# A factor per hidden column: multiplied into the weights, or applied to h as it leaves PSUM

## The chip, the cores and the metric

The kernel runs on one core of one Trainium2 chip. The metric is the device time of one execution in microseconds. A profile's span is about 1.8 us shorter than the device time of the same execution. The engines are TensorE (PE; PEld is its weight load), VectorE (DVE), ScalarE (ACT), GpSimd (POOL) and SyncE (SP; SPq is its queue of transfers).

## The reference, cut to what matters

```python
# attention: batch 8, heads 8, seq 576, head_dim 64; k and v averaged in pools of 8
attn = softmax(scale * q @ k_p^T);  x = (attn @ v_p)          # 4608 tokens x 512
# feed forward: w_in 512 x 2048, w_out 2048 x 512, alpha 2048
h = x @ w_in
s = np.sin(alpha * h)
g = h + s * s / (alpha + 1e-09)
return g @ w_out
```

Everything is float32. The kernel multiplies g by (alpha + 1e-9) and divides the rows of w_out by the same factor. What it forms is therefore (alpha + 1e-9) h + sin²(alpha h), and the question is where that one multiplication by alpha + 1e-9 happens.

## The kernel before

The kernel before scales the columns of w_in, 16 DVE operations, three ahead of the first unit and the others in it, so PSUM already holds the scaled h:

```python
def combine_w_in(self, J, part):                  # J = 0..3; parts 0 and 1
    ...
    def scaled(t, i):
        c = self.alb[:, i * h + J * w:i * h + (J + 1) * w].unsqueeze(1).to_broadcast([P, 2, w])
        nc.vector.tensor_tensor(out=t[:, :, s], in0=t[:, :, s], in1=c, op=OP.mult)
    ...                                           # scaled() for four blocks, then sums of blocks
```

`alb` is alpha + 1e-9 broadcast over the partitions, made at the start with four matmuls. The hidden layer is a product of 2x2 blocks with seven products in place of eight. Tokens come in nine **units** of 512. A unit has four **groups** of 256 hidden columns (J), and a group has seven products, so a unit has 28 **slots**, 0 to 27, of one product each. What a group does after product k stands in the functions `left0` to `left6`:

```python
def left2(G=G, Q=before):                         # Q is the group before
    if Q: self.store_g(Q)                         # SyncE: 1 MB to the bridge tensor in HBM
    G.b7 = bank(); nc.scalar.copy(out=G.b7[:], in_=G.b6[:])
    G.p5 = self.tp.tile([P, JW, TH], F32, name="p5")
    nc.scalar.copy(out=G.p5[:], in_=G.b5[:])      # 128x512
def left3(G=G):
    sin(G, 0, 0, G.b1); square(G, G.s[:, 0, 0])   # Sin with a scale per partition
def left4(G=G): add(G.g[:, 1, 1], G.b7[:], G.p5[:])
def left5(G=G):
    add(G.g[:, 0, 1], G.b6[:], G.p5[:])
    sin(G, 1, 1, G.g[:, 1, 1])
    add(G.g[:, 0, 0], G.b1[:], G.s[:, 0, 0])
```

`G.g` has two buffers, which take turns, and is what `store_g` sends. Beside the hidden products the attention of the **next** batch is made, in fixed slots:

```python
for i in range(5):                                # five tiles of tokens, units 1 to 6
    at((1, 3, 4, 5, 6)[i], A.score, i)            # PE; DVE takes max and subtracts it
    at(8 + (i + 1) // 2, A.exp, i)                # ACT
    at(9 + (i + 1) // 2, A.norm, i)               # DVE sums, GpSimd multiplies
    at((12, 12, 13, 14, 14)[i], A.turn, i)        # DVE transposes blocks into tr
at(14, A.move, 0); at(15, A.move, 1)              # SyncE: aT <- tr, 2 x 6 transfers
...
    at(24, A.values, hp)                          # four products of aT with v; ACT copies them into x
at(24, A.values_rest)
...                                               # turn_q, DVE, writes tr again from slot 21 on
```

Score tiles, and the products with v, share a ring of three PSUM buffers.

## Time and profile before

| | us |
|---|---|
| median of the runs (957.71 to 959.04) | 958.2 |
| span of the profile | 956.4 |
| first hidden product | 38.2 |
| unit 0 | 38.2 to 115.3 |
| units 1 to 6, sum | 343.0 |
| mean of units 1 to 5 | 57.22 |

A unit is measured in the trace from the start of the first matmul of its first product to the same in the next unit; all unit and slot times below are worked out so. Three things are to be read from the profile before: PE is full from unit 1 on, DVE bounds the last half of unit 0, and units 1 to 6 have almost the same length. The lines that carry this are in the prediction.

### The profile page before, as it was taken

Reading aid. Unit: us, or ns where it says so; the run is one execution under the profiler, and the core shown is the slowest. Engines: PE = TensorE matmul, PEld = TensorE weight load, DVE = VectorE, ACT = ScalarE, POOL = GpSimd, SP = SyncE. Lnnn points to the kernel's source line nnn. Section 1 sums busy time; section 2 is a strip of 40 time slices with the busy share of each in tenths; the row PEclk is TensorE's granted clock in tenths of the full one; section 3 lists DMA queues with packets and bytes.
Section 4 is the critical chain, followed back from the end, with each engine's and each line's share of the span. In section 5 each row is a group of like instructions: output and inputs, shape, how many; then the busy total and the mean of one; then the engine's idle time right before and its main releaser. Section 6 shows DMA issues by size and latency. Waiting matters only on the chain.

```text
span 956.4 us, 18152 instructions
## 1 busy us (share of the span) xinstructions
PE 937.6 (98%) x7259; PEld 833.4 (87%) x7259; DVE 676.5 (71%) x1070; ACT 414.2 (43%) x919; POOL 197.7 (21%) x215
## 2 busy tenths in 40 slices
PE   7998999999999999999999999999999999999998
PEld 3677687887878878787888899999999999999998
DVE  5889585766838577483576996867768695958684
ACT  5376466575756747566555531111111111111111
POOL 1717364443724436260000000000000000000000
PEclk9999999999999999999999999999999999999999
DMA  9636466666576663745615235324142434343201
GB/s 222 176 104 198 125 195 142 205 149 196 171 198 201 156 190 102 188 136 161 242 54 206 98 142 190 125 102 161 67 155 78 143 115 147 98 139 122 100 34 35
DMA packets 84038, 137.88 MB, mean 144 GB/s; under 512 B 10177, under 2 KB 49873, under 8 KB 79345
## 3 DMA queue, kind: packets, MB, share of 16 engines
q1 hardware_dynamic: 83920, 136.70, 47.1%
q8 instruction: 58, 0.95, 0.4%
q14 instruction: 26, 0.21, 0.1%
q10 hardware_dynamic: 34, 0.02, 0.0%
HBM read 74.47 MB, written 47.19 MB: 127 GB/s over the span
## 4 chain that ended last, share of the span: by engine, by line
PE 92%; DVE 4%; ACT 2%; DMA 1%; issue 0%; SPq 0%; DVEq 0%; ACTq 0%
PE bank L489 42%; PE bank L752 30%; PE ps_y L752 12%; PE ps_o L309 3%; PE ps_sc L208 2%; DMA q<-in_q_dram 1%; DVE as L368 1%; ACT s L495 1%; PE ps_at L267 1%; DVE home L462 1%; DVE a L372 1%; PE ps_qt L189 1%; PE bank L452 1%; DVE h L468 0%; PE ps_or L318 0%
## 5 line engine op out<-in xcount | busy, mean ns | idle before, releaser
L489 PE MATMUL bank<-home,a 128*128 128x256 f32 x1152 | 266.3, 382 | 3.0 <-DVE h L468 1.6
L489 PEld LDWEIGHTS bank<-home,a 128*128 128x128 f32 x1152 | 215.3, 190 | 36.6 <-DVE h L468 3.1
L489 PE MATMUL bank<-home,as 128*128 128x256 f32 x864 | 201.6, 382 | 2.8 <-DVE as L368 1.6
L489 PEld LDWEIGHTS bank<-home,as 128*128 128x128 f32 x864 | 161.7, 190 | 26.7 <-ACT bank L507 2.4
L105 POOL TENSOR_TENSOR kvin<-kvin 72x512 f32<-72x512 f32 x112 | 126.0, 1125 | 180.3 <-DMA kvin<-in_v_dram 112.0
L495 ACT ACTIVATE s<-h,rat 128x256 f32<-128x256 f32 x144 | 65.2, 500 | 90.2 <-DVE h L468 90.2
L468 DVE TENSOR_TENSOR h<-bank,p 128x512 f32<-128x512 f32 x72 | 49.1, 682 | 74.7 <-ACT s L497 47.4
L752 PE MATMUL bank<-wb,home 128*128 128x128 f32 x712 | 92.1, 275 | 0.0
L752 PEld LDWEIGHTS bank<-wb,home 128*128 128x128 f32 x712 | 85.7, 192 | 0.0
L831 ACT COPY bank<-bank 128x128 f32<-128x128 f32 x63 | 15.8, 250 | 149.3 <-PE bank L752 149.2
L497 ACT ACTIVATE s<-s 128x512 f32<-128x512 f32 (+1 forms) x106 | 77.8, 768 | 1.1
L495 ACT ACTIVATE s<-bank,rat 128x256 f32<-128x256 f32 x144 | 59.9, 467 | 36.9 <-PE bank L489 24.4
L752 PE MATMUL bank<-wb,xe 128*128 128x128 f32 x512 | 67.6, 275 | 0.0
L752 PEld LDWEIGHTS bank<-wb,xe 128*128 128x128 f32 x512 | 62.4, 192 | 0.1
L844 ACT COPY bank<-bank 128x128 f32<-128x128 f32 x63 | 15.8, 250 | 96.6 <-PE bank L752 96.6
L250 POOL TENSOR_TENSOR ex<-ex,sm 128x576 f32<-128x576 f32 (+1 forms) x38 | 42.5, 1148 | 46.5 <-DVE sm L249 21.4
L549 DVE TENSOR_TENSOR h<-h,s 128x1024 f32<-128x1024 f32 x36 | 44.5, 1237 | 0.0
L549 DVE TENSOR_TENSOR h<-bank,s 128x512 f32<-128x512 f32 x36 | 24.5, 681 | 24.5 <-ACT s L497 23.9
L819 ACT COPY bank<-ps_y 128x256 f32<-128x256 f32 x63 | 22.5, 357 | 35.9 <-PE ps_y L752 35.9
L519 ACT COPY bank<-bank 128x512 f32<-128x512 f32 x36 | 20.6, 571 | 39.4 <-PE bank L489 39.4
L712 DVE TENSOR_TENSOR xe<-home 128x512 f32<-128x512 f32 x30 | 19.4, 687 | 25.5 <-PE bank L752 25.4
L215 DVE TENSOR_REDUCE mx<-ps_sc 128x4 f32<-128x288 f32 (+1 forms) x75 | 33.6, 448 | 4.4 <-PE ps_sc L208 4.4
(152 smaller groups left out, 1499.3 us busy)
## 6 DMA issues: line engine op xcount, KB each, us to landing
g_bridge<-h SPq DMA_DIRECT2D x36, 1024.0 KB
r<-g_bridge SPq DMA_DIRECT2D x18, 1024.0 KB
home<-g_bridge SPq DMA_DIRECT2D x18, 1024.0 KB
out_dram<-o SPq DMA_DIRECT2D x36, 256.0 KB
q<-in_q_dram SPq DMA_DIRECT2D x8, 1024.0 KB
kvin<-in_k_dram SPq DMA_DIRECT2D x28, 288.0 KB
kvin<-in_v_dram SPq DMA_DIRECT2D x28, 288.0 KB
a<-in_moe_w_in_dram SPq DMA_DIRECT2D x16, 256.0 KB
```

The lines of the kernel that those rows point to most:

```text
L105: (eng or nc.gpsimd).tensor_tensor(out=o, in0=t[:, :, 0:w], in1=t[:, :, w:2 * w], op=OP.add)
L215: nc.vector.tensor_reduce(out=mx[:n], in_=ps[:n], axis=AX, op=OP.max)
L250: eng.tensor_tensor(out=E(n, i, 0, H), in0=E(n, i, 0, H), in1=sm[:n].unsqueeze(2).to_broadcast([n, H, Sp]), op=OP.mult)
L309: nc.tensor.matmul(ps[64 * e:64 * e + 64, :], vp[:, h, :], x, start=True, stop=True)
L468: add = lambda o, x, y: nc.vector.tensor_tensor(out=o, in0=x, in1=y, op=OP.add)
L489: nc.tensor.matmul(ps[:, jj, :], self.A[p][:, kk, f * P:(f + 1) * P], x[:, kk, :], start=(start and jj == 0 and kk == 0), stop=(kk == 1), ...
L495: nc.scalar.activation(out=G.s[:, i, j, jj, :], in_=src[:, jj, :], func=AF.Sin, scale=self.rat[:, f:f + 1])
L497: square = lambda G, x: nc.scalar.activation(out=x, in_=x, func=AF.Square)
L519: nc.scalar.copy(out=G.b7[:], in_=G.b6[:])
L549: add = lambda o, x, y: nc.vector.tensor_tensor(out=o, in0=x, in1=y, op=OP.add)
L752: nc.tensor.matmul(out, A[:, J, :], W[:, J // 2, J % 2, :], start=(start and J == 0), stop=(J == self.NJ - 1), skip_group_check=True)
L819: nc.scalar.copy(out=x[:, 0:2, :], in_=yz[:, 0:1, :].to_broadcast([P, 2, P]))
```

## The change

The intent: take the 16 scalings, and the broadcast of alpha, out of the start, where DVE is the bound. In their place ACT's copies of one PSUM bank and DVE's adds, which read PSUM anyway, take alpha + 1e-9 as a scale per partition. Five groups of slots were moved too. The diff, cut to its core:

```diff
-    def load_alpha(self, row, rows): ...     # alb: alpha + 1e-9 broadcast over partitions
+    def load_alpha(self, rows): ...          # al, ale = al + 1e-9, ral = 1/ale, rat = al/ale
...
 def combine_w_in(self, J, part):
-        def scaled(t, i): ...                # and its 16 uses
...
             def left2(G=G, Q=before):
-                G.p5 = self.tp.tile([P, JW, TH], F32, name="p5")
-                nc.scalar.copy(out=G.p5[:], in_=G.b5[:])
+                for i in (1, 0):
+                    for jj in range(JW):
+                        f = self.chunk(G, i, jj)
+                        nc.scalar.activation(out=G.g[:, i, 1, jj, :], in_=G.b5[:, jj, :], func=AF.Identity, scale=self.ale[:, f:f + 1])
...
             def left4(G=G):
-                add(G.g[:, 1, 1], G.b7[:], G.p5[:])
+                self.scale_add(G, 1, 1, G.b7, G.g[:, 1, 1])
...                                           # the other two adds, and one in finish(), the same way
+    def scale_add(self, G, i, j, h, x):
+        for jj in range(JW):
+            f = self.chunk(G, i, jj)
+            self.nc.vector.scalar_tensor_tensor(out=G.g[:, i, j, jj, :], in0=h[:, jj, :], scalar=self.ale[:, f:f + 1],
+                                                in1=x[:, jj, :], op0=OP.mult, op1=OP.add)
...                                           # unit 0
-            at(6, A.k_t)
+            at(7, A.k_t)
-                at((7, 8, 9, 11, 13)[i], A.score, i)
+                at((8, 9, 10, 11, 13)[i], A.score, i)
...                                           # units 1 to 6
-                at(9 + (i + 1) // 2, A.norm, i)
-                at((12, 12, 13, 14, 14)[i], A.turn, i)
+                at((9, 10, 10, 12, 12)[i], A.norm, i)
+                at((13, 13, 13, 14, 14)[i], A.turn, i)
...
-                at(24, A.values, hp)
-            at(24, A.values_rest)
+                at(24 + hp // 2, A.values, hp)
+            at(25, A.values_rest)
```

More of the change, by code (lines that the diff above doesn't have):

```diff
@@ L321, in attention, with load_alpha, turn_alpha @@
         return SimpleNamespace(**{f.__name__: f for f in (k_t, q_t, score, exp, score_exp, norm, new_a, a_t, turn, move, values, values_rest)})
-    def load_alpha(self, row, rows):
+    def load_alpha(self, rows):
         nc = self.nc
-        self.al = self.const.tile([P, self.K2], F32, name="al")
-        self.ral = self.const.tile([P, self.K2], F32, name="ral")
-        self.rat = self.const.tile([P, self.K2], F32, name="rat")
-        self.alb = self.new_tr()[:, 0:self.FF]
-        self.al_row, self.al_rows = row[0:1], rows[:self.K2]
+        self.al, self.ale, self.ral, self.rat = (self.const.tile([P, self.K2], F32, name=n) for n in ("al", "ale", "ral", "rat"))
+        self.al_rows = rows[:self.K2]
         nc.scalar.dma_start(out=self.al_rows, in_=self.alpha.rearrange("(k p) -> k p", p=P))
-        nc.scalar.dma_start(out=self.al_row, in_=self.alpha.rearrange("(o n) -> o n", o=1))
-    def combine_alpha(self):
+    def turn_alpha(self):
         nc = self.nc
@@ L340, in combine_alpha @@
         nc.scalar.copy(out=self.al[:], in_=ps[:])
-        for c in range(4):
-            s = slice(512 * c, 512 * c + 512)
-            ps = self.bank([P, 512], c)
-            nc.tensor.matmul(ps[:], self.ones[:], self.al_row[:, s], start=True, stop=True)
-            nc.scalar.activation(out=self.alb[:, s], in_=ps[:], func=AF.Identity, bias=self.ex[:, 0, 0, self.Sp:self.Sp + 1])
-        nc.vector.tensor_scalar(out=self.ral[:], in0=self.al[:], scalar1=1e-9, scalar2=None, op0=OP.add)
-        nc.vector.reciprocal(out=self.ral[:], in_=self.ral[:])
+        nc.vector.tensor_scalar(out=self.ale[:], in0=self.al[:], scalar1=1e-9, scalar2=None, op0=OP.add)
+        nc.vector.reciprocal(out=self.ral[:], in_=self.ale[:])
         nc.vector.tensor_tensor(out=self.rat[:], in0=self.al[:], in1=self.ral[:], op=OP.mult)
@@ L368, in combine_w_in @@
         tt = lambda o, x, y, op: nc.vector.tensor_tensor(out=o[:, :, s], in0=x[:, :, s], in1=y[:, :, s], op=op)
-        def scaled(t, i):
-            c = self.alb[:, i * h + J * w:i * h + (J + 1) * w].unsqueeze(1).to_broadcast([P, 2, w])
-            nc.vector.tensor_tensor(out=t[:, :, s], in0=t[:, :, s], in1=c, op=OP.mult)
-        if J < 2:
-            if part == 0:
-                scaled(a11, 0)
-                scaled(a21, 1)
-                scaled(a22, 1)
-                tt(s1, a21, a22, OP.add)
-            else:
-                tt(s2, s1, a11, OP.subtract)
-                scaled(a12, 0)
-                tt(a21, a11, a21, OP.subtract)
-                tt(s4, a12, s2, OP.subtract)
-        elif part == 0:
-            for t, i in ((a11, 0), (a21, 1), (a22, 1), (a12, 0)):
-                scaled(t, i)
+        if part == 0:
+            tt(s1, a21, a22, OP.add)
         else:
-            tt(s1, a21, a22, OP.add)
             tt(s2, s1, a11, OP.subtract)
@@ L490, in product, with sin @@
                                          start=(start and jj == 0 and kk == 0), stop=(kk == 1), skip_group_check=True)
-            def sin(G, i, j, src):
+            def sin(G, i, j, src, by):
                 for jj in range(JW):
-                    f = i * self.K2 // 2 + G.J * JW + jj
-                    nc.scalar.activation(out=G.s[:, i, j, jj, :], in_=src[:, jj, :], func=AF.Sin, scale=self.rat[:, f:f + 1])
+                    f = self.chunk(G, i, jj)
+                    nc.scalar.activation(out=G.s[:, i, j, jj, :], in_=src[:, jj, :], func=AF.Sin, scale=by[:, f:f + 1])
             square = lambda G, x: nc.scalar.activation(out=x, in_=x, func=AF.Square)
@@ L519, in left2 @@
                 nc.scalar.copy(out=G.b7[:], in_=G.b6[:])
-                G.p5 = self.tp.tile([P, JW, TH], F32, name="p5")
-                nc.scalar.copy(out=G.p5[:], in_=G.b5[:])
+                for i in (1, 0):
+                    for jj in range(JW):
+                        f = self.chunk(G, i, jj)
+                        nc.scalar.activation(out=G.g[:, i, 1, jj, :], in_=G.b5[:, jj, :], func=AF.Identity, scale=self.ale[:, f:f + 1])
             def left3(G=G):
-                sin(G, 0, 0, G.b1)
+                sin(G, 0, 0, G.b1, self.al)
                 square(G, G.s[:, 0, 0])
             def left4(G=G):
-                add(G.g[:, 1, 1], G.b7[:], G.p5[:])
+                self.scale_add(G, 1, 1, G.b7, G.g[:, 1, 1])
             def left5(G=G):
-                add(G.g[:, 0, 1], G.b6[:], G.p5[:])
-                sin(G, 1, 1, G.g[:, 1, 1])
-                add(G.g[:, 0, 0], G.b1[:], G.s[:, 0, 0])
+                self.scale_add(G, 0, 1, G.b6, G.g[:, 0, 1])
+                sin(G, 1, 1, G.g[:, 1, 1], self.rat)
+                self.scale_add(G, 0, 0, G.b1, G.s[:, 0, 0])
             def left6(G=G):
-                sin(G, 0, 1, G.g[:, 0, 1])
-                sin(G, 1, 0, G.b7)
+                sin(G, 0, 1, G.g[:, 0, 1], self.rat)
+                sin(G, 1, 0, G.b7, self.al)
                 if early(G):
@@ L547, in finish, with chunk @@
     def finish(self, Q):
-        nc = self.nc
-        add = lambda o, x, y: nc.vector.tensor_tensor(out=o, in0=x, in1=y, op=OP.add)
-        add(Q.g[:, 1, 0], Q.b7[:], Q.s[:, 1, 0])
-        add(Q.g[:, :, 1], Q.g[:, :, 1], Q.s[:, :, 1])
+        self.scale_add(Q, 1, 0, Q.b7, Q.s[:, 1, 0])
+        self.nc.vector.tensor_tensor(out=Q.g[:, :, 1], in0=Q.g[:, :, 1], in1=Q.s[:, :, 1], op=OP.add)
+    def chunk(self, G, i, jj):
+        return i * self.K2 // 2 + G.J * JW + jj
+    def scale_add(self, G, i, j, h, x):
+        for jj in range(JW):
+            f = self.chunk(G, i, jj)
+            self.nc.vector.scalar_tensor_tensor(out=G.g[:, i, j, jj, :], in0=h[:, jj, :], scalar=self.ale[:, f:f + 1],
+                                                in1=x[:, jj, :], op0=OP.mult, op1=OP.add)
     def store_g(self, Q):
@@ L572, in first_batch @@
         h = [self.hp.tile([P, 4 * POOL * self.D], F32, name="h") for _ in range(2)]
-        self.load_alpha(h[1][:], self.hp.tile([P, P], F32, name="s", bufs=1)[:])
-        self.combine_alpha()
+        self.load_alpha(self.hp.tile([P, P], F32, name="s", bufs=1)[:])
+        self.turn_alpha()
         for i in range(4):
@@ L858, in run @@
             make_identity(nc, ident)
-            self.ones = const.tile([1, P], F32, name="ones")
-            nc.gpsimd.memset(self.ones[:], 1.0)
             engines = {nc.tensor.engine, nc.vector.engine, nc.scalar.engine, nc.gpsimd.engine, nc.sync.engine}
```

## The prediction

> **What bounds the kernel now.** I read the strips of the page first, then the chain that ended last, then the sums by stretch, and last the order of time on TensorE (PE), VectorE (DVE) and ScalarE (ACT) in the stretch that looked worst. From the page:
>
> ```profile
> PE 937.6 (98%) x7259; PEld 833.4 (87%) x7259; DVE 676.5 (71%) x1070; ACT 414.2 (43%) x919; POOL 197.7 (21%) x215
> ...
> PE   7998999999999999999999999999999999999998
> PEld 3677687887878878787888899999999999999998
> DVE  5889585766838577483576996867768695958684
> ...
> PE 92%; DVE 4%; ACT 2%; DMA 1%; issue 0%; SPq 0%; DVEq 0%; ACTq 0%
> ```
>
> PE is busy nearly always and makes 92% of the chain; what is not PE lies in the first five slices (a slice is 24 us), where DVE reaches 8 and 9. So the kernel has three stages: a start up to about 115 us, hidden products on PE up to about 560 us, output products after that. The sums by stretch (columns: PE, PEld, DVE, ACT, POOL busy) say how they differ:
>
> ```profile
> 62.89:80.92 18.03, 17.03 (x154) 13.88 (x148) 17.53 (x31) 8.98 (x19) 6.09 (x7) 1.00 0.79 234
> 80.92:98.36 17.44, 13.79 (x73) 11.39 (x73) 16.71 (x24) 13.85 (x24) 14.51 (x13) 1.00 0.48 132
> 98.36:113.61 15.25, 15.25 (x94) 10.62 (x93) 7.76 (x11) 7.23 (x19) 6.33 (x8) 1.00 0.42 129
> 113.61:300.00 186.39, 186.39 (x1442) 152.37 (x1441) 125.23 (x216) 117.03 (x230) 85.80 (x93) 1.00 0.66 179
> ```
>
> From 62.89 to 98.36 DVE is busy 34.2 of 35.5 us: it is the bound there. After 113.61 PE has no idle time, DVE is at 67% and ACT at 63%. In that stage one product of the hidden layer is 8 matmuls, and two in a row take 3.45 us from start to start, so 1.73 each. A unit of 512 tokens is 28 products; its stores to the bridge tensor come 57.2 to 57.5 us apart. The first unit takes from 38.21 to 115.3, that is 77.1 us. It does more: ten groups of transposes of the attention (about 0.43 each), five of q (0.55), the leftovers of batch 0 (about 1.4), 8.5 in all. 57.3 + 8.5 = 65.8, so **PE loses about 11.3 us in the first unit**. That is all a relief of DVE and ACT could win.
>
> **What the Trainium skill says, and whether the trace agrees.**
> "VectorE: DVE Perf Modes", section on the TRN2 errata: a float32 tensor_tensor takes (N+151)/0.96 ns, so 691 for 512 and 424 for 256; the trace has 682 and 415. It gives no figure for scalar_tensor_tensor; I take it as a tensor_tensor of its size.
> The same table: ScalarE from PSUM takes (172+FD)/1.2 ns, so 357 for 256 and 570 for 512. The trace has 357 and 571 for plain copies, but 467 for a Sin of 256 whose scale is read per partition, and 687 for an Identity of 512 with a bias read per partition: about 110 more.
> "SBUF — State Buffer", section "SBUF: two separate sides": a DVE operation with two SBUF inputs and a GpSimd operation that reads SBUF exclude each other for a whole instruction. The trace agrees: four scalings of w_in took 2.49 us at one place and 4.56 at another where GpSimd was busy. The new fused operation reads one input from PSUM, so by this it is not held up.
> "ScalarE: Activation LUTs", "Table sets: the hidden batching unit": cheap functions, identity among them, are in every set. The two kernels' lists of instructions agree: both have 16 table loads, so the new Identity adds none.
>
> **The change, part by part.** The times by line, shapes kept apart (count | busy us, mean ns):
>
> ```profile
> L495 ACT ACTIVATE s<-bank,rat 128x256 f32<-128x256 f32 x144 | 59.9, 467 | 36.9 <-PE bank L489 24.4 <-issue 8.8 <-DVE h L549 1.2
> L468 DVE TENSOR_TENSOR h<-bank,p 128x512 f32<-128x512 f32 x72 | 49.1, 682 | 74.7 <-ACT s L497 47.4 <-PE bank L489 20.0 <-issue 6.6
> L521 ACT COPY p<-bank 128x512 f32<-128x512 f32 x36 | 21.2, 589 | 0.0
> L372 DVE TENSOR_TENSOR a<-a,tr 128x512 f32<-128x512 f32 x16 | 12.7, 842 | 0.0
> ```
>
> 1. Removed on DVE: the 16 scalings of w_in, 12.7 us (mean 842, against 0.62 where GpSimd is quiet), all before 84.1 us.
> 2. Removed at the very start: 4 broadcasts of alpha through PE (7.2 us) and 4 ACT activations (2.7 us). They end before 13.5 us, when q lands, and the chain runs through that transfer. Worth 0.
> 3. Added on DVE: 144 adds of 128x512 (36 groups, 4 each, 98.1 us) become 288 fused operations of 128x256, by 415 ns 119.5 us: **+21**. Starts of 512-wide adds lie 0.60 us apart, so two of 256 take about 0.07 more than one of 512, 0.28 per group of 7 products (12.1 us).
> 4. Added on ACT: 36 copies of 128x512 (21.2 us) become 144 scaled copies of 128x256 by 467 ns, 67 us. With part 2: **+43**. In a row two Sins take 0.84, so four take about 1.58 in place of the copy's 0.5: **+1.05 per group** in ACT's queue.
> 5. Moved: k^T of batch 1, its scores, and from unit 1 on the normalizing, turning and half of the products with v, by up to two slots. No work changes.
>
> So the sums should read DVE 676.5 - 12.7 + 21.4 = 685 and ACT 414 + 43 = 457. Both rise, while the time should fall, because only the early part is on the path.
>
> **What lies on the path in the first unit.** In order of time on PE, and then on DVE and ACT:
>
> ```profile
> 80.92 1.99 PE L489 MATMUL bank<-home,as 128*128 128x256 f32 x8 [1.00 <-ACT bank L507]
> ...
> 89.89 1.99 PE L489 MATMUL bank<-home,a 128*128 128x256 f32 x8 [1.62 <-DVE h L468]
> ...
> 97.39 1.14 PE L267 MATMUL ps_at<-ident,ex 128*72 128x128 f32 x8 [2.02 <-DVE aT L269]
> ```
> ```profile
> 68.25 2.49 DVE L372 TENSOR_TENSOR a<-a,tr 128x512 f32<-128x512 f32 x4
> ...
> 76.58 0.68 DVE L468 TENSOR_TENSOR h<-bank,p 128x512 f32<-128x512 f32 x1
> ...
> 79.47 4.56 DVE L372 TENSOR_TENSOR a<-a,tr 128x512 f32<-128x512 f32 x4
> ```
> ```profile
> 77.29 0.91 ACT L495 ACTIVATE s<-h,rat 128x256 f32<-128x256 f32 x2 [3.29 <-DVE h L468]
> ```
>
> The add at 76.58 comes late because DVE's queue is full; Sin at 77.29 waited 3.29 us for it, and PE at 80.92 for ACT. I followed the new queues by hand. From 38 to 60 us one scaling (1.13) leaves the path ahead of batch 0's last scores, but the scaled copies put 1.05 back into ACT's queue, which is full there: 0. At 55.75 PE waited 0.81 for a buffer of k^T; one slot later it doesn't, and product and scores close up: +2.2 us by slot 8. Slots 8 to 16: 2.49 less on DVE, of which PE can use about 1.0, plus about 0.9 from the late add: 4.1 by slot 16. Slots 16 to 22: 4.56 go, but ACT is now nearly full (exponentials, two table loads, one more scaled group of 1.05), and the normalizing still waits for the exponentials: 2 to 3 more. From 98.36 on PE is full already: 0. **Sum: about 6 of the 11.3.**
>
> **What it costs later.** In the steady units the tight place is the exponentials: ACT has them between two table loads, with the copy of b5 in their midst, 1.05 longer. There the next Sin waited 0.71 us for DVE, so 0.3 remains, and the copy that PE needs next ended 0.9 us early; PE shouldn't see it. I charge 0.1 us a unit for it, 8 units: about 0.8. The output stage has none of the changed instructions: 0. 958.2 - 6 + 0.8 = **953.0 us**.
>
> **Rivals.** (a) ACT becomes the bound of the steady stage: it rises from 63% to about 72%, in bursts. If the copies between banks came late by 0.5 us in each of 32 groups, +16 us, so about 968. Against it: ACT shows waits on DVE or PE in nearly every group (90.2 us of waits of Sin on DVE in all). (b) ACT takes DVE's place in the first unit and the win shrinks to 1 or 2 us, 956 to 957; for it: ACT is busy 13.85 of 17.44 us after 80.92. (c) Nearly all lost time of the first unit comes back: 948. Against it: the wait of 1.64 us at 44.41 for s2 stays, since sums of x stand ahead of it in DVE's queue, and so do GpSimd's conflicts with the last combination. (d) The scaled copies write the bridge's staging buffer two slots earlier and could wait for the store of the group two before; stores of 1 MB are done some 5 us after issue, and 12 us lie between. I give it little.
>
> **Range and chances.** Rival (b) gives the upper end, most of (c) the lower: 949 to 957.5. Faster by over 2% would need 19 us, more than PE loses in the start; slower needs rival (a) in full. Faster 0.01, same 0.98, slower 0.01.
>
> **What would show it.** The sums of DVE and ACT near 685 and 457, with the fused operation near 415 ns and the scaled copy near 467. The bridge stores of the first unit earlier by about 6 us, of which 2 by the second product of its second group; then 57.2 to 57.5 us per unit, and the output stage as long as before. In 62 to 98 us, DVE no longer full and ACT nearly so. Wrong would be: units of 58 us or more, with waits of PE on ACT's copies; or a fused operation of over 0.5 us.

## The result, and the profile after

The changed kernel took 961.78 us (median of 4 runs, 961.04 to 963.18) against 958.21 (957.71 to 959.04) for the kernel before in the same rounds. The ratio is 1.0038, 95% interval 1.0021 to 1.0055. All ratios here are the mean time of one kernel's fast runs over the mean of the other's fast runs of the same rounds, so they are not quite the ratios of the medians. Executions over 1.5% slower than the fastest of the same kernel are left out of the means. The change costs 0.4%, and the prediction, 949 to 957.5, does not hold it.

From the page of the changed kernel: the sums, DVE's strip, the chain that ended last, and the new groups (count | busy us, mean ns | idle before, releaser):

```profile
PE 935.5 (97%) x7251; PEld 833.1 (87%) x7251; DVE 691.7 (72%) x1198; ACT 442.0 (46%) x1023; POOL 204.4 (21%) x214
...
DVE  5779684857848677485586997868768685958684
...
PE 87%; DMA 5%; SPq 3%; ACT 2%; DVE 2%; issue 1%; POOL 0%; DVEq 0%; POOLq 0%
...
L536 DVE SCALAR_TENSOR_TENSOR h<-bank,ale,h 128x256 f32<-128x256 f32 x144 | 62.4, 475 | 69.2 <-PE bank L464 25.8
...
L499 ACT ACTIVATE h<-bank,ale 128x256 f32<-128x256 f32 x144 | 56.4, 478 | 13.2 <-DMA g_bridge<-h 13.2
```

The chain is the line to stop at. Before, transfers made 1% of it and SyncE's queue nothing. Now transfers make 5% and SyncE's queue 3%: the path leaves PE and runs through transfers, which no part of the change adds. The last line shows a second new thing, 13.2 us in which ACT's scaled copies waited for a store to the bridge.

The sums by stretch of the changed kernel (PE, PEld, DVE, ACT, POOL busy) answer to those in the prediction:

```profile
62.90:80.90 18.00, 17.47 (x149) 14.12 (x147) 17.14 (x33) 11.60 (x23) 8.74 (x9) 1.00 0.79 239
80.90:98.40 17.50, 16.09 (x93) 12.96 (x94) 16.27 (x28) 12.66 (x25) 16.45 (x16) 1.00 0.54 176
98.40:109.51 11.11, 11.11 (x69) 7.66 (x66) 2.28 (x6) 6.44 (x19) 0.79 (x2) 1.00 0.44 109
109.51:286.39 176.88, 173.73 (x1261) 141.27 (x1260) 122.46 (x240) 120.21 (x252) 85.13 (x87) 1.00 0.63 173
```

In the two stretches up to 98.4 us PE is busy for 33.6 us, against 30.8 before, and unit 0 ends at 109.5 instead of 115.3. The last line covers units 1 to 3: PE, which had no idle time there before, is idle for 3.2 of 176.9 us. So the balance of the two spans (956.4 and 960.4) is this: unit 0 ends 5.8 us earlier, units 1 to 6 take 352.7 instead of 343.0 us, that is 9.7 more, and the rest is equal to 0.3 us.

**Where in a unit.** The table gives the mean of units 1 to 5, in us. "Slots 8–13" runs from the first matmul of slot 8 to that of slot 14, and so on. "Slot 4" runs from the first matmul of slot 3 to that of slot 4, since the extra work of a slot stands ahead of its product; when the text says that PE waits in slot 4, 11 or 13, it means ahead of that slot's product. The experiments named x1, x3, x5 and x6 are told below. Slots not listed agree within 0.1.

| kernel | unit 0 ends at | unit | slot 4 | slots 8–13 | slots 23, 24 | slots 25–27 |
|---|---|---|---|---|---|---|
| before | 115.34 | 57.22 | 2.60 | 10.40 | 7.70 | 5.48 |
| after | 109.51 | 59.05 | 3.17 | 10.36 | 8.91 | 5.59 |
| x1: old slots for normalizing | 109.81 | 59.27 | 3.15 | 11.55 | 7.94 | 5.59 |
| x3: new slots alone | 114.55 | 57.84 | 2.61 | 10.36 | 8.25 | 5.59 |
| x5: fused operations alone | 117.63 | 57.79 | 2.99 | 10.58 | 7.70 | 5.48 |
| x6: scaled copies alone | 116.31 | 58.61 | 2.74 | 11.37 | 7.99 | 5.48 |

The unit grew by 1.83 us: 0.57 in slot 4, 1.21 in slots 23 and 24, 0.11 after them. Not all of the last two is a wait: x1, where PE does not wait for the transfer, still has 7.94 and 5.59 against 7.70 and 5.48, so the split of the products with v over two slots costs 0.35 us by itself, and 0.97 is left for the transfer.

**Slots 23 and 24.** First the kernel before, in order of time, with the transfers that fill aT, the store of the second group, the transpose of q that reuses tr, and the first product with v:

```profile
261.97 3.88 SPq L285 DMA_DIRECT2D aT<-tr  x6
...
271.01 0.69 SPq L554 DMA_DIRECT2D g_bridge<-h  x1
...
274.79 3.02 DVE L145 STREAM_TRANSPOSE tr<-q 128x1024 f32<-128x1024 f32 x4 [4.62 <-DMA aT<-tr]
...
275.68 2.80 PE L309 MATMUL ps_o<-aT,vp 72*64 72x512 f32 x12
```

Then the same place of the changed kernel (its unit starts at 227.7, that of the kernel before at 229.8):

```profile
261.65 3.89 SPq L285 DMA_DIRECT2D aT<-tr  x6
...
270.52 0.39 SPq L540 DMA_DIRECT2D g_bridge<-h  x1
...
274.60 3.02 DVE L145 STREAM_TRANSPOSE tr<-q 128x1024 f32<-128x1024 f32 x4 [5.97 <-DMA aT<-tr]
...
274.72 1.94 PE L309 MATMUL ps_o<-aT,vp 72*64 72x512 f32 x8 [0.95 <-DMA aT<-tr]
...
276.98 1.57 ACT L499 ACTIVATE h<-bank,ale 128x256 f32<-128x256 f32 x4 [2.55 <-DMA g_bridge<-h]
```

Before, DVE already waited 4.62 us for aT to land; nobody saw it, because PE came to the product 0.89 us after that landing. That small distance was the whole slack. Reckoned from the start of the unit and averaged over units 1 to 5, the first move is issued at 32.17 us before and at 34.35 after, 2.2 us later; twelve moves, at about 0.65 us each in SyncE's queue, and the rest of the way to the landing take the same 13 us in both. So PE now stands for the transfer. The last line shows the store: its data were ready at 263.5 (the add that completes them ends then), but it stood behind the moves in SyncE's queue until 270.5, and the scaled copies, which write the same buffer for a later group, could start 6.5 us after that.

**Slot 4.** Again in order of time, first of the kernel before: DVE's last add of the group before, then the first half of score tile 2 taken out of its PSUM buffer, then the next score tile on PE.

```profile
293.24 1.22 DVE L549 TENSOR_TENSOR h<-h,s 128x1024 f32<-128x1024 f32 x1
...
294.85 0.46 DVE L216 TENSOR_TENSOR ex<-ps_sc,mx 128x288 f32<-128x288 f32 x1
...
295.76 0.73 PE L208 MATMUL ps_sc<-kblk,q 64*64 64x72 f32 x32
```

The same of the changed kernel:

```profile
293.18 1.95 DVE L527 TENSOR_TENSOR h<-h,s 128x1024 f32<-128x1024 f32 x1
...
295.54 0.46 DVE L216 TENSOR_TENSOR ex<-ps_sc,mx 128x288 f32<-128x288 f32 x1
...
296.10 0.72 PE L208 MATMUL ps_sc<-kblk,q 64*64 64x72 f32 x30 [0.61 <-issue]
```

GpSimd, which pools v meanwhile, in the kernel before and then in the changed one:

```profile
293.39 2.99 POOL L105 TENSOR_TENSOR kvin<-kvin 72x512 f32<-72x512 f32 x2 [11.42 <-DMA kvin<-in_v_dram]
```
```profile
292.79 2.93 POOL L105 TENSOR_TENSOR kvin<-kvin 72x512 f32<-72x512 f32 x2 [10.81 <-DMA kvin<-in_v_dram]
```

Counted from the start of unit 4 (287.0 before, 286.4 after), the buffer comes free 1.3 us later. About 0.55 of that are three fused pairs ahead of it in DVE's queue; 0.73 is the add of 128x1024, which the change did not touch and which took 1.95 us in place of 1.22. In the kernel before, GpSimd began 0.15 us after that add, in the changed one 0.39 us ahead of it. In the changed kernel the add takes 1.38, 2.19 and 1.95 us in units 1, 2 and 4, where a GpSimd operation was under way when it began, and 1.21 to 1.22 in units 3, 5 and 6, where none was; in the kernel before it is long in unit 1 alone (1.66). Where the add is short, slot 4 takes 2.79 us against 2.58. So the fused operations are worth about 0.2 us a unit here, and about 0.36 of the 0.57 is this add beside GpSimd, the meeting that the prediction saw at the scalings of w_in and did not look for in the steady units. No run varies GpSimd alone, and the units that it hits differ from kernel to kernel.

PE gets through two of the 32 matmuls of its next score tile and stands for 0.61 us until the buffer is emptied. DVE's queue is full in slots 0 to 4, and each thing that is put into it moves the score buffers.

### The profile page after: what moved, and what is told of

Same layout as the page of the kernel before. It is cut to its first block, busy times and chain, and to the rows that moved or that the text cites. A ratio compares the mean times of both kernels' runs of the same rounds, so it can differ in the third digit from the quotient of the medians.

```text
span 960.4 us, 18405 instructions
## 1 busy us (share of the span) xinstructions
PE 935.5 (97%) x7251; PEld 833.1 (87%) x7251; DVE 691.7 (72%) x1198; ACT 442.0 (46%) x1023; POOL 204.4 (21%) x214
## 4 chain that ended last, share of the span: by engine, by line
PE 87%; DMA 5%; SPq 3%; ACT 2%; DVE 2%; issue 1%; POOL 0%; DVEq 0%; POOLq 0%
PE bank L464 38%; PE bank L738 29%; PE ps_y L738 11%; PE ps_o L309 3%; PE ps_sc L208 3%; SPq L285 2%; DMA aT<-tr 2%; DMA q<-in_q_dram 1%; DMA a<-in_moe_w_in_dram 1%; DMA home<-g_bridge 1%; DMA kvin<-in_k_dram 1%; PE ps_at L267 1%; PE ps_qt L189 1%; DVE as L359 0%; DVE h L536 0%
## 5 line engine op out<-in xcount | busy, mean ns | idle before, releaser
L536 DVE SCALAR_TENSOR_TENSOR h<-bank,ale,h 128x256 f32<-128x256 f32 x144 | 62.4, 475 | 69.2 <-PE bank L464 25.8
L536 DVE SCALAR_TENSOR_TENSOR h<-bank,ale,s 128x256 f32<-128x256 f32 x144 | 62.0, 471 | 16.4 <-ACT s L472 16.4
L470 ACT ACTIVATE s<-bank,al 128x256 f32<-128x256 f32 x144 | 60.5, 476 | 16.1 <-PE bank L464 11.1
L499 ACT ACTIVATE h<-bank,ale 128x256 f32<-128x256 f32 x144 | 56.4, 478 | 13.2 <-DMA g_bridge<-h 13.2
L527 DVE TENSOR_TENSOR h<-h,s 128x1024 f32<-128x1024 f32 x36 | 46.2, 1283 | 0.0
L145 DVE STREAM_TRANSPOSE tr<-q 128x1024 f32<-128x1024 f32 (+1 forms) x24 | 18.1, 808 | 29.4 <-DMA aT<-tr 23.0
```

The costliest lines, as they stand in the source:

```text
L470: nc.scalar.activation(out=G.s[:, i, j, jj, :], in_=src[:, jj, :], func=AF.Sin, scale=by[:, f:f + 1])
L499: nc.scalar.activation(out=G.g[:, i, 1, jj, :], in_=G.b5[:, jj, :], func=AF.Identity, scale=self.ale[:, f:f + 1])
L527: self.nc.vector.tensor_tensor(out=Q.g[:, :, 1], in0=Q.g[:, :, 1], in1=Q.s[:, :, 1], op=OP.add)
L536: self.nc.vector.scalar_tensor_tensor(out=G.g[:, i, j, jj, :], in0=h[:, jj, :], scalar=self.ale[:, f:f + 1], in1=x[:, jj, :], op0=OP.mult, ...
```

## The experiments

Two theories stood at the start. **Theory A**: the loss in units 1 to 6 comes from the new arithmetic (longer queues on ACT and DVE) that delays the chain of attention: exponentials, normalizing, turning, moves, product with v. **Theory B**: it comes from the slots that the change moved. **Theory C** is rival (d) of the prediction: the scaled copies wait for the bridge store. (The expectations call them theory 2, theory 1 and theory 3.) Thirteen kernels were run. All gave correct results but x11. The totals of x2, x4, x9, x10 and x12 came out slower than any case that their expectations named.

One thing alters how the times of x2, x4, x10 and x12 are read: in those profiles **the granted clock of TensorE fell to 0.50** for stretches that began after PE had stood still. From the sums by stretch of x2 (the third number from the right is the clock), where PE stood for 1.52 us up to 225.82:

```profile
224.00:226.00 2.00, 0.48 (x4) 0.21 (x4) 2.00 (x5) 2.00 (x8) 1.21 (x1) 0.85 0.18 42
226.00:228.00 2.00, 2.00 (x13) 0.82 (x14) 0.39 (x1) 0.99 (x5) 1.92 (x2) 0.50 0.56 131
228.00:230.00 2.00, 2.00 (x16) 1.64 (x13) 0.00 (x0) 0.87 (x3) 0.77 (x2) 0.50 0.60 140
```

Added up in windows of 1 us up to the last few us of the span, (1 − clock) makes 15.4 us in x2, 8.5 in x4, 8.5 in x10 and 5.1 in x12, always in lots of 1.71 us: half the clock for 3.4 us. In the profiles of before, after, x1, x3, x7, x9, x11 and x13 it is 0; in x5, x6 and x8 it is one lot, in unit 0. So unit 0 of x5 and x6 in the table has 1.7 us that belongs to the clock. Where a unit is quoted "without the clock's part" below, these lots are taken off it; that is an estimate, exact only if PE had work throughout.

**x1. The old slots for normalizing and turning, with the new arithmetic.**

```diff
-                at((9, 10, 10, 12, 12)[i], A.norm, i)
-                at((13, 13, 13, 14, 14)[i], A.turn, i)
+                at(9 + (i + 1) // 2, A.norm, i)
+                at((12, 12, 13, 14, 14)[i], A.turn, i)
```

> The changed kernel with one part undone: from unit 1 on, normalizing and turning stand in their old slots (turns from slot 12, not 13); the products with v stay split. Theory 1 (the later turns start the moves of aT about 2.5 us later, their issue takes 13.5 us, and PE waits for them at slot 24): units 1 to 6 fall from 58.5 to 59.6 us to about 57.5 to 58.0, total about 955 to 957. Theory 2 (the extra ScalarE work delays everything, and the later slots only follow it): units stay at 58.5 or grow, total 961 or more. Theory 3 (the scaled copies wait 2.4 us for the store of the bridge at slot 24): units fall by under 0.5 us.

Measured: 965.1 us, ratio to before 1.0066 (1.0051 to 1.0081). Slots 23 and 24 fall to 7.94 us, but slots 8 to 13 rise to 11.55. There PE waits for DVE in slot 13 of every unit, as in unit 4:

```profile
315.45 3.72 PE L464 MATMUL bank<-home,a 128*128 128x256 f32 x16 [0.93 <-DVE h L536]
```

So the new slots are not the fault; they are a trade. With the new arithmetic in the old slots the fused add stands behind the normalizing and PE loses 1.15 us in slots 8 to 13. With the new slots this is gone, and 0.97 more is lost at the transfer.

**x2. All products with v in slot 24 again.**

```diff
-                at(24 + hp // 2, A.values, hp)
-            at(25, A.values_rest)
+                at(24, A.values, hp)
+            at(24, A.values_rest)
```

> The changed kernel with another part undone: all products with v in slot 24 again. Theory 1: no gain, since the first of them waits for the same transfer; unit length within 0.5 us of the changed kernel's, total 960 to 964. If the split itself cost the time, units would fall to about 57.5 and the total to 955. Theory 3: the copies of x behind the waiting scaled copies now hold up more products, so units grow by 1 to 2 us.

Measured: 987.86 us (976.98 to 993.61; the fast ones are 976.98, 986.05 and 989.68), ratio 1.0259 (1.0181 to 1.0336). Units of 63.05 us, 60.3 without the clock's part. On ACT, in unit 2, the scaled copies and behind them the copies of the products into x:

```profile
223.60 1.57 ACT L499 ACTIVATE h<-bank,ale 128x256 f32<-128x256 f32 x4 [2.38 <-DMA g_bridge<-h]
225.05 1.77 ACT L300 ACTIVATE home<-ps_o 128x320 f32<-128x320 f32 x6
```

The scaled copies stand 2.38 us for the store. The fourth product needs one of the three buffers that the copies into x empty, and starts at 225.82, after 1.52 us of idle time. So theory C reaches PE here, where all four products stand in one slot. The split over two slots was necessary with the new arithmetic, and 15.4 us of the 24 us that this kernel's span is longer than that of after are the clock's.

**x3. The kernel before with the new slots of units 1 to 6 alone.** 

```diff
-                at(9 + (i + 1) // 2, A.norm, i)
-                at((12, 12, 13, 14, 14)[i], A.turn, i)
+                at((9, 10, 10, 12, 12)[i], A.norm, i)
+                at((13, 13, 13, 14, 14)[i], A.turn, i)
-                at(24, A.values, hp)
-            at(24, A.values_rest)
+                at(24 + hp // 2, A.values, hp)
+            at(25, A.values_rest)
```

> The kernel before with only the new slots of units 1 to 6 (normalizing, turning, products with v later), arithmetic as before. Theory 1: units grow from 57.2 to about 58 to 59 without any of the new ScalarE work, total 963 to 968 (no gain in the first unit). Theory 2: units stay at 57.2, total 958.

Measured: 961.42 us, ratio 1.0034 (1.0019 to 1.0050). The unit grows by 0.62 us, all of it in slots 23 and 24 (0.55) and after (0.11). The moves are issued 1.07 us later. This is theory B, and it is about a third of the loss; 0.35 of the 0.62 is the split itself (x1), the rest a wait of PE for the transfer.

**x4. The scaled copies written into the other tile, which no store reads.**

```diff
-  nc.scalar.activation(out=G.g[:, i, 1, jj, :], in_=G.b5[:, jj, :], func=AF.Identity, scale=self.ale[:, f:f + 1])
+  nc.scalar.activation(out=G.s[:, i, 1, jj, :], in_=G.b5[:, jj, :], func=AF.Identity, scale=self.ale[:, f:f + 1])
```

The adds read `G.s` accordingly.

> The changed kernel, scaled copies of b5 written into the free half of the tile s, not into the tile that the bridge store of two groups before still reads. The wait of ScalarE on that store (13.2 us in six places) should go. Theory 3: units 1 to 6 fall by 1 to 2 us each, total 950 to 956. Theory 1: they fall by 0 to 0.5 us each, total 959 to 962.

Measured: 985.7 us, ratio 1.0271 (1.0225 to 1.0317); units of 63.23 us, 61.5 without the clock's part. The wait for the store is gone and a longer one has its place:

```profile
290.74 1.57 ACT L499 ACTIVATE s<-bank,ale 128x256 f32<-128x256 f32 x4 [5.21 <-DVE h L527]
```

`G.s` has one buffer, and DVE's last read of it by the group before stands in DVE's queue behind the transpose that waits for aT. So the experiment did not take theory C away; it replaced it with a wait on the same late transfer, and is no verdict on how much the store costs.

**x5. The fused operations alone**, in the kernel before, with a scale of 1.0.

```diff
-                add(G.g[:, 1, 1], G.b7[:], G.p5[:])
+                self.scale_add(G, 1, 1, G.b7, G.p5)
```

The three other adds from PSUM change the same way.

> The kernel before, its slots and its scalings kept; only the 144 adds of 128x512 become 288 fused operations of 128x256 with a scale of 1.0 (result unchanged). A fused one took 472 ns in the changed kernel, two start 0.79 us apart against 0.60 for the add, so 0.76 us more per group. Theory DVE-late (VectorE, full in slots 0 to 4 of each unit, empties score buffers late): the interval at slot 4 grows from 2.6 to 2.8 or more in units 1 to 6, slot 24 by about 0.3, units 57.6 to 58.2, total 961 to 965. If the fused operations hide, units stay 57.2 and the total 958 to 959.

Measured: 960.12 us, ratio 1.0013 (0.9991 to 1.0036). In its trace the unit grows by 0.57 us: 0.39 in slot 4, where x3 had nothing, and 0.18 in slots 8 to 13. In units 1, 3, 4 and 5 slot 4 takes 2.79 us against 2.58 to 2.68 before, which the fused operations explain; in unit 2 it takes 3.78, and there the add of 128x1024 took 2.21 us, begun while GpSimd was busy. So the fused operations are one cause of slot 4 and not the only one: half of the 0.39 is that one add. The profiled run (963.2 us) was the slowest of the four and the timed interval contains 1, so how much of it every run pays stays open. The fused operations take 474 ns each, and a pair starts 0.79 us apart from what follows, against 0.60 for one 512-wide add.

**x6. The scaled copies alone**, in the kernel before, with a scale of 1.0: four of 256 columns, written to p5.

```diff
-                nc.scalar.copy(out=G.p5[:], in_=G.b5[:])
+                for i in (1, 0):
+                    for jj in range(JW):
+                        nc.scalar.activation(out=G.p5[:, jj, :], in_=G.b5[:, jj, :], func=AF.Identity, scale=self.one[:, jj:jj + 1])
```

> The kernel before, its slots, scalings and adds kept; only the copy of b5 becomes four scaled copies (scale 1.0), into the old separate tile, so no wait for the bridge store. Theory ACT-late (1.05 us more between the exponentials delays the normalizing, and the add behind it in VectorE's queue holds up the product of slot 13): the interval at slot 13 grows from 1.7 to about 2.8 as in x1, the turns and with them slot 24 come later by 0.5 to 1.0; units 58.5 to 59.5, total 966 to 972. If only the store wait and the slots matter: units 57.2 to 57.5, total 958 to 960.

Measured: 968.03 us, ratio 1.0095 (1.0074 to 1.0116). This is the costliest single part: the unit grows by 1.39 us, of which 0.97 in slots 8 to 13, 0.29 in slots 23 and 24, and 0.14 in slot 4 (an add lengthened beside GpSimd in units 1 and 2). The 0.29 is no wait for the transfer, since PE comes 1.10 us later to the product with v, as much as the moves do: in unit 4 the four products take 3.94 us in place of 3.65, and the copies into x, behind the scaled copies, start 2.07 us after the first product in place of 1.13. In slots 10 to 12 of unit 4, with the new copies between the exponentials:

```profile
315.36 1.55 ACT L525 ACTIVATE p<-bank,one 128x256 f32<-128x256 f32 x4
...
317.58 0.76 DVE L257 TENSOR_REDUCE sm<-ex 128x8 f32<-128x584 f32 x1 [1.04 <-ACT ex L225]
```

The copies end at 316.9; the last two exponentials follow them; DVE's normalizing waits 1.04 us for these, and the add into which PE's next product accumulates stands behind the normalizing. PE waits 0.74 us for it in slot 13, at 320.06. This was what the prediction declared hidden.

**x7. Neither kernel's way.** w_in stays unscaled and so does w_out. ACT's Square takes the factor: Square of sqrt(1/(alpha + 1e-9)) times the sine is sin²/(alpha + 1e-9), which is the reference's own form. The copy of b5 and the adds are plain and 512 wide again, and the old slots of units 1 to 6 are back.

```diff
+        nc.scalar.activation(out=self.rs[:], in_=self.rs[:], func=AF.Sqrt)      # rs held 1/(alpha + 1e-9)
...
+    def square(self, G, i, j=None):
+        for jj in range(JW):
+            f = self.chunk(G, i, jj)
+            x = G.s[:, i, :, jj, :] if j is None else G.s[:, i, j, jj, :]
+            self.nc.scalar.activation(out=x, in_=x, func=AF.Square, scale=self.rs[:, f:f + 1])
```

> Another way to leave w_in unscaled: h is used as it comes, Sin takes alpha as its scale, and the Square takes the root of 1/(alpha+1e-9) as its scale per partition, so the adds stay plain and 512 wide, b5 has its one plain copy, w_out needs no scaling; old slots in units 1 to 6, k^T of batch 1 in the new one. ScalarE has about 0.65 us more per group, VectorE nothing. If the first unit's gain comes from the scalings alone and the loss from the fused adds, the store wait and the slots: first unit 72 us, units 57.2 to 58.0, total 951 to 957, faster than both. If any extra ScalarE work costs a unit over 1 us: 958 or more.

Measured: 956.40 us (955.39 to 957.92), ratio to before 0.9970 (0.9952 to 0.9989). It beats both kernels. Unit 0 ends at 108.3, units take 57.75 us, and slots 4, 23 and 24 are as in the kernel before; slots 8 to 13 take 10.95 us against 10.40. (The root needs a positive alpha; the reference's inputs have at least 0.5.) From its page:

```profile
PE 934.2 (98%) x7251; PEld 829.7 (87%) x7251; DVE 657.0 (69%) x1021; ACT 439.7 (46%) x1027; POOL 197.6 (21%) x214
...
PE 94%; ACT 2%; DVE 2%; DMA 1%; issue 0%; SPq 0%; DVEq 0%; ACTq 0%
```

PE makes 94% of the chain again and SyncE's queue none. ACT is as busy as in the changed kernel (439.7 and 442.0 us), so ACT's sum is not what made the changed kernel slow: there the added work stood between the exponentials and ahead of the moves.

**x8. k^T of batch 1 in its old slot**, in the changed kernel.

```diff
-            at(7, A.k_t)
+            at(6, A.k_t)
-                at((8, 9, 10, 11, 13)[i], A.score, i)
+                at((7, 8, 9, 11, 13)[i], A.score, i)
```

> The changed kernel with k^T of batch 1 and its first three score tiles back in their old slots, all else as changed. If moving it gave part of the gain in the first unit: the wait of about 0.8 us at slot 6 comes back, first unit 72.5 to 74 against 72.1, total 962 to 964. If it gave nothing: 72.1 and 961.8.

Measured: 962.62 us, ratio 1.0035 (1.0007 to 1.0064), as much as the changed kernel's own. Unit 0 ends at 110.46 instead of 109.51, but it contains one lot of half clock (1.7 us) after a gap of 1.92 us at 52.85. Without it there is no gain from the later slot to be seen, save that this gap is gone.

**x9. x7 with all squares at the start of the next group** instead of some of them early.

```diff
-            early = lambda G: G.J == (0 if G.u else 1)
+            early = lambda G: False
```

> As x7, but the squares of the group before the exponentials stay behind the copy that PE needs next (in x7 they stand ahead of it, and slots 8 to 13 are each 0.1 to 0.2 us longer than before). If that copy is what is late in x7: those intervals return to 1.7, units 1 to 6 fall from 57.7 to 57.2 to 57.4, total about 953, faster than the kernel before by about 0.5%. If not: 956 as in x7.

Measured: 962.38 us, ratio 1.0036 (1.0022 to 1.0051). Slots 8 to 13 rise to 11.95 us, because the copy between banks at slot 10 comes late and PE waits 1.15 us in slot 11 of every unit. The order of x7 is better. (Of the 1.36 us that its units are longer than those of x7, 1.00 is here; 0.37 is in slot 4, with the add lengthened beside GpSimd in units 1, 2 and 5, though this kernel has no fused operations.)

**x10. The store of the second group issued by ACT**, in the changed kernel, so that it doesn't stand behind the moves.

```diff
-        self.nc.sync.dma_start(out=self.gd[Q.u, Q.J], in_=...)
+        (self.nc.scalar if 0 < Q.u < self.B - 1 and Q.J == 1 else self.nc.sync).dma_start(out=self.gd[Q.u, Q.J], in_=...)
```

> The changed kernel; the one bridge store per unit that stands behind the moves of aT in SyncE's queue (second group, units 1 to 6) is issued from ScalarE's queue instead, some 7 us earlier. Theory store-late: ScalarE's wait for it (13.2 us) goes, SyncE has one transfer less to issue ahead of the rest, slots 23 and 24 fall by 0.5 to 1.0 us, units to about 58, total 956 to 959. If that wait was hidden: units as in the changed kernel, 961 to 963.

Measured: 984.25 us, ratio 1.0280 (1.0242 to 1.0318); units of 63.14 us, 61.4 without the clock's part. The store is issued 7.3 us earlier (36.1 us into the unit instead of 43.4), and then shares the transfer engines with the moves: the last move is issued at 45.6 us instead of 42.5, and aT lands 2.6 us later. PE waits for it:

```profile
285.48 1.96 PE L309 MATMUL ps_o<-aT,vp 72*64 72x512 f32 x8 [2.87 <-DMA kvin<-in_k_dram]
```

(The profile names the transfer that came last, a load of k that is not an input of this product.) The store also stands in ACT's own queue until DVE's add has completed its data (270.91 in unit 3), and the copy between two banks behind it starts 3.37 us late; PE waits 1.19 us for that copy in slot 18. So the experiment has two new costs, and the late store was in effect giving way to the moves.

**x11. The kernel before with the 16 scalings left out** (wrong result, relative error 0.42).

```diff
-            nc.vector.tensor_tensor(out=t[:, :, s], in0=t[:, :, s], in1=c, op=OP.mult)
+            pass
```

> The kernel before with its 16 scalings of w_in left out and nothing else (its result is wrong on purpose). The term of the prediction for the first unit alone: the second unit's first product starts at about 109 to 110 instead of 115.3, later units stay at 57.2, total 952 to 953. If the gain needs the other parts (k^T later): 954 to 956. If the path runs elsewhere: 958.

Measured: 955.78 us, ratio 0.9965 (0.9946 to 0.9984). Unit 0 ends at 111.30 instead of 115.34, and units take 57.20 us. So the scalings cost about 4 us, and a version that only removes them cannot gain much more than that. This rests on one profile of each: x3, whose code is that of the kernel before up to there, ends unit 0 at 114.55, and the timed difference is about 3.3 us (interval 1.5 to 5.2).

**x12. The products with v one slot later still**, in the changed kernel.

```diff
-                at(24 + hp // 2, A.values, hp)
-            at(25, A.values_rest)
+                at(25 + hp // 2, A.values, hp)
+            at(26, A.values_rest)
```

> The changed kernel with the products with v of units 1 to 6 one slot later still (two in slot 25, the rest in 26). If PE waits at slot 24 for the landing of aT, that wait (slots 23 and 24 together 8.9 us against 7.7 before) falls by 0.5 to 1.0 us and the total goes to 957 to 960, unless the next unit's x then comes late (slots 26 to 1 longer by as much). If PE waits there for ScalarE, which waited for the store, the copies of x now stand behind nothing that waits, and slots 25 and 26 are at their pure length. If neither: 962.

Measured: 971.92 us, ratio 1.0137 (1.0108 to 1.0166); units of 60.17 us, 59.14 without the clock's part, beside 59.05 in the changed kernel. In order of time in unit 3, ACT's copies into x:

```profile
283.33 2.51 ACT L300 ACTIVATE home<-ps_o 128x256 f32<-128x256 f32 x8
```

And the products with v on PE in the same unit:

```profile
277.86 1.94 PE L309 MATMUL ps_o<-aT,vp 72*64 72x512 f32 x8
...
284.07 1.08 PE L309 MATMUL ps_o<-aT,vp 72*64 72x512 f32 x4 [1.33 <-POOL kvin L105]
```

The first product no longer waits: the transfer had indeed been what it waited for. But the copies into x, behind the scaled copies that waited 2.46 us for the store, start at 283.33, and the last product stands for 1.33 us. The profile names GpSimd, which is no input of it; that the buffer came free with ACT's copies is read from the order of time.

**x13. x7 with one early square moved ahead of the copy between banks and the other behind it.**

```diff
                 if Q and not early(Q):
                     squares(Q)
+                elif Q:
+                    square(Q, 1)
...
                 if early(G):
-                    squares(G)
+                    square(G, 0, 1)
```

> As x7, with the 0.89 us that ScalarE waits for PE ahead of the copy that PE needs next filled by one of the two early squares, and the other one after the copy (x7 had both ahead, x9 both after). If the order on ScalarE is all that x7 loses in units 1 to 6: 57.2 to 57.5 us instead of 57.75, total 953 to 956. If the later square delays the exponentials as in x9: slot 11 longer, 57.5 to 58.5, total 956 to 960.

Measured: 958.41 us, ratio 0.9994 (0.9981 to 1.0008), units of 58.35 us. It gives back what x7 won. Of the 0.60 us that its units are longer than those of x7, 0.20 is in slots 8 to 13; 0.40 is in slot 4, with the add lengthened beside GpSimd in units 1, 2 and 4, so how much is due to the order stays open.

## Why the prediction was wrong, point by point

**The first unit: right in its sum.** "About 6 of the 11.3" was 5.8, though the terms as written add up to 6.1 to 7.1. The parts were right only in part: what the prediction takes from the scalings (1.9 by slot 16, 2 to 3 more) comes near the 4.0 of x11, while the k^T step, put at 2.2 by slot 8, shows no gain of its own in x8. The remaining 1.8 us was not taken apart, and a good sum is partly luck here: profiles of the same code differ by up to 0.9 us at this point (after, x1, x2, x10 and x12 end unit 0 at 109.1 to 110.0). The clue "DVE no longer full" failed as well: DVE was busy for 33.4 of 35.5 us (34.2 before), but PE got 2.7 us more out of it.

**The cost of the operations: right on ACT, too small on DVE.** Four scaled copies took 1.55 to 1.57 us (1.58 was expected), at 478 ns each (467). The fused operation took 471 to 475 ns in the mean, not 415 (none over 486, so none was held up beside GpSimd, as the prediction said), so a pair cost 0.19 us more than one add, not 0.07. DVE's sum came to 691.7, not 685; 1.7 of the difference is the add of 128x1024 beside GpSimd (46.2 us for 36, against 44.5 before). ACT's came to 442, not 457, for the larger part because count times mean counts the overlap of neighbours twice: 144 copies of 478 ns were busy for 56.4 us, not 68.8. No table load was added, as said.

**The step that failed is "What it costs later".** It charged "0.1 us a unit", 0.8 in all. Units 1 to 6 grew by 9.7 us, and the sign of the result turned on this. It looked at one place only, ACT between the two table loads, and asked whether PE's next copy came in time. It should have followed what the exponentials feed. x6 shows that alone: copies that delay two exponentials by about 1 us cost 1.39 us a unit, most of it (0.97) because DVE's normalizing waits and the add that PE needs stands behind it, and 0.29 because the copies into x stand behind the scaled copies; turning and moves start 1.10 us later too. In the changed kernel the new slots took the first of these away, and what was left over came out at the transfer (0.97) and in slot 4 (0.57).

**The moved slots were given no cost.** "No work changes" is true, yet x3 shows 0.62 us a unit from them alone, 0.35 for the split and the rest at the transfer. The slack they spent was to be seen in the profile before: aT landed 0.75 us ahead of its use (mean of units 1 to 5; the transpose of q, which waits for the same transfers, starts at 45.11 us of the unit and the product at 45.86). The three parts alone delay the first move by 1.07 (x3), 0.93 (x5) and 1.10 us (x6), each more than that slack; together by 2.2. In x5 and x6 PE still did not wait there, because the products before had come later themselves, by 0.57 and 1.10 us in the unit.

The parts alone add up to 0.62 + 0.57 + 1.39 = 2.58 us a unit, more than the 1.83 measured. This fits with what the new slots do: they remove what the arithmetic costs in slots 8 to 13 (1.15, x1 against before), and bring a part of it back at the transfer.

**Rival (d), given "little", did happen:** 13.2 us of waits in six places. The sum "stores are done some 5 us after issue, and 12 us lie between" took issue to follow on the data; the store stood 7 us behind the moves in SyncE's queue, and the same was so in the kernel before. x4 and x10 can't say what it cost, since both replaced it with something worse. But the table's kernels can: in units 1 to 5 it ends 49 us or more into the unit, after the first product with v (47.28) has begun, so it can only lengthen what follows, and there the changed kernel takes 4.32 us in slot 24 and 5.59 in slots 25 to 27, x3, which has no such wait, 4.26 and 5.59. So it cost PE about 0.06 us a unit directly. x2 and x12 show that with the products in other slots it does reach PE, through the copies into x.

**Rival (a) was not it.** The prediction's own sign of failure, "units of 58 us or more", came true, but PE did not wait for ACT's copies between banks: it waited for a score buffer that DVE emptied late (slot 4: fused operations, and the add beside GpSimd) and for a transfer (slot 24).

## What to carry to other kernels

An engine at 60 to 70% still has places where a microsecond more in its queue is not hidden: follow what stands behind the added instruction through every engine to the transfer that it delays, and compare the delay with the time between that transfer's landing and its use. Look for a factor's home in an instruction that already takes a scale and stands off that path; here the square did (x7, 0.3% faster than before), while copies amid the exponentials did not. When a variant is much slower than its waits explain, read the granted clock of each stretch before inventing a cause.

## What the Trainium skill lacked or had wrong

- "TensorE: Matmul & The Clock Gate", "Why this matters for your kernels", says to leave no idle gaps of TensorE above about 3 us between bursts of matmuls. Here the clock fell to 0.50 after gaps as short as 1.21 us (x2), and 1.33 and 0.92 us (x12), though not after every such gap: one of 2.02 us in the profile of the kernel before did nothing. The length of a spell, 3.4 us (1.71 us lost) or twice that, agrees with the window of 3413 ns that the page gives in its Part 1.
- "VectorE: DVE Perf Modes", the section on the TRN2 errata, has no figure for scalar_tensor_tensor. With 256 columns, one input in PSUM and the scalar read per partition it took 471 to 475 ns, against 415 for a tensor_tensor of that shape.
- "DMA: Bandwidth & Descriptors", "Issuing engines are not separate DMA queues", calls the time to start a transfer usually small beside the transfer. Here twelve moves of a few partitions each took 3.9 and 4.2 us per six in SyncE's queue, 8 us in all; one move's 0.65 us is small beside the 4.2 us from the last issue to the landing (unit 3), but a store that was ready waited 7 us behind all of them. That transfers from two queues share the same engines agrees: x10's store, issued by ACT, made aT land 2.6 us later.
